# New durations and delays in the planner that orders an attention and mixer kernel

## The chip, the cores and the metric

The kernel runs on one core of a Trainium2 chip. The core has five engines with an instruction list each: TensorE (PE, matrix products, with its weight loads shown as PEld), VectorE (DVE), ScalarE (ACT), GpSimd (POOL) and SyncE (SP, which issues all transfers between memory and the core). An engine works through its list in order; a semaphore holds an instruction back until what it needs is there. The metric is the device time of one execution in microseconds (us). The kernel before took 1168.48 us, the median of three runs (1167.81 to 1168.57).

## The reference

Eight batches, eight heads, 576 positions, head size 64. The attention is block-causal: a query sees the keys of its own block of 64 and of the blocks before it.

```python
scores = (1/8) * q @ k^T, masked by blocks of 64      # per batch and head, 576 x 576
attn   = softmax(scores)
x      = attn @ v, heads side by side                 # 8 x 576 x 512
u      = x + (x^T @ U @ V)^T                          # U: 576 x 32, V: 32 x 576, over the positions
out    = u + relu(u @ w_ch1) @ w_ch2                  # w_ch1: 512 x 2048, w_ch2: 2048 x 512
```

U, V, w_ch1 and w_ch2 come as 64-bit floats (f64), q, k and v as 32-bit ones.

## The kernel before

**Stages.** A loop over the 64 heads writes the attention. A head is five tiles of up to 128 queries: products of queries and keys on PE (L1185 as full 32-bit products for heads 0 to 11, L1189 and L1190 as rounded products of two parts for the others), the row maximum on DVE (L1203), the exponential with its row sum on ACT (L1214), sum and reciprocal on DVE (L1230, L1231), the scaling on POOL (L1240), transposes on PE (L1273), a high part on ACT (L1250) and the rest on DVE (L1292, and L1299 which moves 64 partitions to the other 64), and the product with v on PE (L1316 for heads 0 to 9, L1332 later). The two halves of that product are added through a copy across partitions on ACT (L1338) and a sum on DVE (L1340). After every second head `mix` applies U and V (L1358 to L1408): transposes, splits (L1361, L1363), the product with U (L1372), a short chain over 32 partitions (L1375 to L1379), the product with V (L1387) and the sum u (L1392), which goes to memory.

Beside the heads run the conversion of the f64 weights and the feed-forward products. `split64` turns a block of 512 columns into 32-bit floats: a fetch, a magnitude on ACT (L359), a clamp on POOL (L362), then a shift (L338) and two joins of bits (L343, L351) on DVE. `weights_of` finds a common power of two by a short chain (`power`, L397 to L423) and writes high and low 16-bit halves (ACT L455, DVE L459). When the second half of w_ch2 is there, `agree` reconciles the scales (L482 to L488) and `level` rescales the first half (L499). `ffn_chunk` (288 tokens each) splits u (L596, L600, or L609, L614, L615), multiplies by the first half of the 2048 hidden columns (L631), applies the relu (L636, L639), multiplies by w_ch2 (L656) and adds (L668). These products are PE's stock of spare work: their priority number is over a million, the heads' at most 64 thousand, so PE takes them when no step of a head is ready.

The other 1024 hidden columns come last, in `block_products` (products L873), as two by two blocks with seven products in place of eight; their weights are made by L732, L737, L738 and L741, and the sums around the products are on DVE (L802, L810, L820, L827) and ACT (L801, L805, L834, L940).

**What sets the order.** Nothing is issued by hand. Each step is a task with an engine, an expected duration in ns, a priority, what it reads and what it writes. `Plan.issue` simulates the five engines with these numbers and writes each engine's list in the order of that simulation: a free engine takes, among the tasks whose inputs it believes ready, the one with the lowest priority number. The chip then follows the list, whatever the true times. A result of engine e reaches a task on another engine x after the duration, plus `TAIL[e]`, plus `INTO[x]`; on the same engine after 130 ns (for PE at once). DVE tasks marked `port` and all POOL tasks are never simulated at the same time. `_act`, `_dve` and `_pe` give a duration from the number of columns:

```python
TAIL = {"PE": 165, "DVE": 78, "ACT": 105, "POOL": 20, "SP": 0}
INTO = {"PE": 355, "DVE": 35, "ACT": 35, "POOL": 310, "SP": 60}
def _act(n, sbuf=False): return (93 if sbuf else 52) + 0.833 * n
def _dve(n): return 69 + 1.042 * n
```

In the trace a duration on DVE, ACT or POOL also holds the drain of the engine, which the planner counts as `TAIL`; an engine's next instruction can start during the drain of the last.

Of the kernel before, what the change touches and what calls it, by code (L numbers as in the profile page):

```python
# [53 lines left out]
INTO = {"PE": 355, "DVE": 35, "ACT": 35, "POOL": 310, "SP": 60}  # L54
# [192 lines left out]
def _dve(n):  # L247
    return 69 + 1.042 * n
# [13 lines left out]
def attention_then_mixer(  # L262
# [60 lines left out]
    def split64(fetches, shape, hi, lo, dst, prio, gate=(), part=slice(None), whole=None):  # L323
# [32 lines left out]
        if len(shape) > 2:  # L356
# [4 lines left out]
            "POOL", 250 + 0.85 * n, prio,  # L361
# [3 lines left out]
        add("DVE", 130 + 0.55 * n, prio, shift, [st, zt], [zt], port=True)  # L365
        add("DVE", 100 + 1.15 * n, prio, put_upper, [st, zt], [zt], port=True)
# [69 lines left out]
    def weights_of(half_bufs, hi, lo, blocks, scale, prio, limit=None):  # L436
# [15 lines left out]
        for n, b in enumerate(half_bufs["out"]):  # L452
# [5 lines left out]
                "DVE", 150 + 1.3 * CW, last,  # L458
# [15 lines left out]
    def agree(prio):  # L474
# [103 lines left out]
    def ffn_chunk(c, w, wb, fr=range(FC), turn=0):  # L578
# [12 lines left out]
        for k in range(KC):  # L591
            uh, ul = uh_r[k], ul_r[k]
            if not b:
                add(
                    "ACT", _act(T, True), E,
# [3 lines left out]
                    "DVE", _dve(T), E,  # L599
# [5 lines left out]
            else:  # L605
                us = take(us_r, "us")
                add(
                    "POOL", 250 + 0.85 * T, E,
# [6 lines left out]
                add("POOL", 780, E, lambda us=us, h=uh, l=ul: nc.gpsimd.tensor_sub(l.ap, us.ap, h.ap), [us, uh], [ul])  # L615
# [64 lines left out]
    def block_products():  # L680
# [38 lines left out]
        def weights(slots, by, sc):  # L719
# [15 lines left out]
            def halves(x, b):  # L735
                hi, lo, h, l = slots[x]
                add("ACT", _act(1024, True), L, lambda: nc.scalar.copy(hi(), w(b)), [b], [h])  # L737
                add("POOL", 60 + 2.3 * 1024, L, lambda: nc.gpsimd.tensor_sub(lo(), w(b), hi()), [b, h], [l])  # L738

            def total(out, x, y, op):  # L740
                add("POOL", 60 + 2.3 * 1024, L, lambda: getattr(nc.gpsimd, op)(w(out), w(x), w(y)), [x, y], [out])  # L741
# [54 lines left out]
        def piece(x, sc):  # L796
# [3 lines left out]
            if sc is None:  # L800
# [4 lines left out]
                "ACT", _act(2 * T, True), E, lambda: nc.scalar.activation(h.ap, x[0](), AF.Copy, scale=sc[:, 0:1]), [x[1], sc],  # L805
# [23 lines left out]
        def copied(out, x, iv=None):  # L829
            if iv is None:  # L830
# [3 lines left out]
                "ACT", _act(2 * T), E, lambda: nc.scalar.activation(out[0](), x[0](), AF.Copy, scale=iv.ap), [x[1], iv], [out[1]]  # L834
# [325 lines left out]
    def softmax(h, tiles, pr):  # L1160
# [37 lines left out]
        else:  # L1198
            add("PE", _pe(*ns, m=ms) + 40, pr, products, [q1, k1, q2, k2], [bank])
# [24 lines left out]
    def normalise(h, tiles, pr):  # L1224
# [9 lines left out]
        for i in tiles:  # L1234
# [4 lines left out]
                "POOL", 250 + 0.85 * w, pr,  # L1239
# [12 lines left out]
    def transpose(h, g, part, pr):  # L1252
# [41 lines left out]
        if m < n:  # L1294
# [3 lines left out]
                "DVE", _dve(64), pr,  # L1298
# [3 lines left out]
    def apply_v(h, g, pr):  # L1302
# [6 lines left out]
        if h < FP:  # L1309
# [11 lines left out]
            add("PE", cost + 15, pr, whole_products, [vr, *pt.parts], [bank], hold=[xb])  # L1321
# [15 lines left out]
        add("PE", cost + 80, pr, products, [vs, *ph.parts, *pl.parts], [bank], hold=[xb, tmp])  # L1337
        add("ACT", _act(n), pr, lambda: nc.scalar.copy(tmp[0:64, :n], bank[64:P, :n]), [bank], [tmp])  # L1338
# [5 lines left out]
    def mix(p, pr):  # L1344
# [3 lines left out]
        for rows, js in ((P, range(4)), (64, range(4, 5))):  # L1348
# [6 lines left out]
            def products(view=view, js=js, rows=rows):  # L1355
# [7 lines left out]
                "DVE", _dve(n * P), pr, lambda hi=hi, lo=lo, view=view: nc.vector.tensor_sub(lo, view(), f32(hi)),  # L1363
# [11 lines left out]
        add("ACT", _act(P), pr, lambda: nc.scalar.copy(tb.ap, low[R : 2 * R, 0:P]), [bank], [tb])  # L1375
        add("DVE", _dve(P), pr, lambda: nc.vector.tensor_add(tz.ap, low[0:R, 0:P], tb.ap), [bank, tb], [tz])
        add("ACT", _act(P, True), pr, lambda: nc.scalar.copy(t3[0:R, :], tz.ap), [tz], [t3])
        add("POOL", 360, pr, lambda: nc.gpsimd.tensor_sub(t3[R : 2 * R, :], tz.ap, f32(t3[0:R, :])), [tz, t3], [t3])
        add("ACT", _act(P, True), pr, lambda: nc.scalar.copy(t3[2 * R :, :], tz.ap), [tz], [t3])  # L1379
# [123 lines left out]
```

## Time and profile before

| | before |
|---|---|
| profiled execution, its own time | 1168.67 us |
| span of its trace | 1166.9 us |
| PE busy | 1135.2 us (97%) |
| DVE busy | 958.3 us (82%) |
| ACT busy | 794.0 us (68%) |
| POOL busy | 524.2 us (45%) |
| mean granted PE clock | 0.993 |

The span runs from the first to the last instruction; the execution's own time holds 1.8 us more around it. Busy times are unions of the recorded instructions. A PE that is busy in nearly all of the span can be shortened by filling its idle time alone, as long as its work stays the same. In the page, "out<-in" names the written and the read tiles without buffer numbers, "x" a count; in a row of the timeline the bracket gives the engine's idle time before the instruction and what ended it.

### The profile page before, as it was taken

The page shows a single profiled execution, that of the slowest core. Times are in us where ns is not written, and L with a number is a line of the kernel's source. Part 1 is how long each engine was busy: PE and PEld are TensorE (multiplying, and loading weights), DVE is VectorE, ACT ScalarE, POOL GpSimd, SP SyncE. Part 2 cuts the span into 40 slices and gives each one's busy share as a digit, 9 for nine tenths or more (in the row PEclk, how much of TensorE's full clock was granted, in tenths as well). Part 3 has the DMA queues.
Part 4 walks back from the last instruction along what each step waited for, and adds up shares of the span by engine and source line. Part 5 has one row for each costly group of instructions (what it writes and reads, how often), then busy time and mean ns, then how long its engine had stood idle before and what let it go on. Part 6 is the DMA issues. An engine that isn't in the chain of part 4 may idle for free.

```text
span 1166.9 us, 25406 instructions
## 1 busy us (share of the span) xinstructions
PE 1135.2 (97%) x9044; PEld 934.4 (80%) x9044; DVE 958.3 (82%) x2129; ACT 794.0 (68%) x1936; POOL 524.2 (45%) x696
## 2 busy tenths in 40 slices
PE   9999997999999999999999999999999999999998
PEld 7777776877888888888888887777777777777777
DVE  6899998889887878787878773372599999999998
ACT  7878887887898888888788954325345455554543
POOL 5445554876767685858576736737200000000000
PEclk9999997999999999999999999999999999999999
DMA  5454552735443434434433312241303422331321
GB/s 142 135 146 128 152 165 83 210 114 145 119 125 103 116 105 118 110 105 114 115 101 102 94 47 72 88 134 51 102 32 92 122 62 62 122 112 34 101 82 41
DMA packets 75885, 122.70 MB, mean 105 GB/s; under 512 B 8944, under 2 KB 52976, under 8 KB 75760
## 3 DMA queue, kind: packets, MB, share of 16 engines
q1 hardware_dynamic: 75760, 121.09, 36.4%
q8 instruction: 71, 1.16, 0.4%
q14 instruction: 54, 0.44, 0.1%
HBM read 76.23 MB, written 29.49 MB: 91 GB/s over the span
## 4 chain that ended last, share of the span: by engine, by line
PE 70%; DVE 13%; ACT 12%; issue 3%; POOL 1%; DMA 0%; SPq 0%; ACTq 0%; DVEq 0%; POOLq 0%
PE bb L873 28%; PE bf L656 9%; PE bf L631 8%; PE ba L1273 5%; ACT p L1214 5%; PE ba L1332 4%; PE bg L656 3%; PE bg L631 3%; DVE mx L1203 3%; DVE pl L1292 2%; PE ba L1316 2%; PE ba L1189 1%; ACT ph L1250 1%; PE ba L1190 1%; DVE xt L1340 1%
## 5 line engine op out<-in xcount | busy, mean ns | idle before, releaser
L1240 POOL TENSOR_SCALAR p<-p,rv 128x576 f32<-128x576 f32 (+4 forms) x320 | 170.6, 548 | 125.9 <-DVE rv L1231 91.6
L1273 PE MATMUL ba<-ident,p 128*128 128x128 f32 x768 | 123.1, 276 | 7.0 <-ACT p L1214 2.2
L1214 ACT ACTIVATE p<-ba,mx 128x448 f32<-128x448 f32 (+3 forms) x248 | 114.5, 465 | 22.3 <-DVE mx L1203 17.7
L1292 DVE TENSOR_TENSOR pl<-ba,ph 128x512 fp32r<-128x512 f32 x216 | 113.7, 550 | 14.8 <-ACT ph L1250 12.6
L656 PEld LDWEIGHTS <-w2h 128*128 128x128 f16 x1024 | 100.5, 98 | 29.7 <-issue 3.7
L873 PE MATMUL bb<-hh,w1l 128*128 128x288 f16 x448 | 118.9, 286 | 0.0
L873 PE MATMUL bb<-hh,w2h 128*128 128x288 f16 x448 | 118.9, 286 | 0.0
L873 PE MATMUL bb<-hh,w2l 128*128 128x288 f16 x448 | 118.9, 286 | 0.0
L873 PE MATMUL bb<-hh,w1h 128*128 128x288 f16 x448 | 118.9, 286 | 0.0
L656 PE MATMUL bf<-hh,w2h 128*128 128x288 f16 x408 | 118.2, 290 | 0.4 <-DVE ot L668 0.4
L631 PEld LDWEIGHTS <-w1h 128*128 128x128 f16 x1024 | 97.6, 98 | 25.5 <-issue 1.7
L656 PE MATMUL bf<-hl,w2h 128*128 128x288 f16 x408 | 117.3, 288 | 0.0
L656 PE MATMUL bf<-hh,w2l 128*128 128x288 f16 x408 | 117.3, 288 | 0.0
L801 ACT CAST hh<-hb 128x576 f16<-128x576 f32 x96 | 63.6, 666 | 66.8 <-DVE hb L827 43.0
L873 PEld LDWEIGHTS <-w1h 128*128 128x128 f16 x896 | 87.7, 98 | 22.0
L873 PEld LDWEIGHTS <-w2h 128*128 128x128 f16 x896 | 87.7, 98 | 22.0
L1250 ACT CAST ph<-ba 128x512 fp32r<-128x512 f32 x216 | 98.6, 493 | 9.6 <-PE ba L1273 8.1
L1273 PEld LDWEIGHTS ba<-ident,p 128*128 128x128 f32 x768 | 90.1, 142 | 13.7 <-issue 7.8
L1203 DVE TENSOR_REDUCE mx<-ba 128x1 f32<-128x448 f32 (+3 forms) x248 | 94.1, 405 | 4.7 <-PE ba L1190 3.2
L1332 PE MATMUL ba<-ph,vs 128*128 128x256 f32 (+3 forms) x432 | 93.2, 272 | 1.8 <-DVE pl L1292 1.5
L873 PE MATMUL bb<-hl,w2h 128*128 128x288 f16 x448 | 91.6, 286 | 0.0
L873 PE MATMUL bb<-hl,w1h 128*128 128x288 f16 x448 | 91.6, 286 | 0.0
(193 smaller groups left out, 3197.0 us busy)
## 6 DMA issues: line engine op xcount, KB each, us to landing
raw<-in_qk_dram SPq DMA_DIRECT2D x63, 288.0 KB, 3.9
st<-in_w_dram SPq DMA_DIRECT2D x32, 512.0 KB, 3.8
o_d<-ot SPq DMA_DIRECT2D x72, 144.0 KB, 1.8
vr<-in_v_dram SPq DMA_DIRECT2D x32, 320.0 KB, 3.8
ur<-u_d SPq DMA_DIRECT2D x64, 144.0 KB, 2.5
wr<-o_d SPq DMA_DIRECT2D x32, 288.0 KB, 3.1
out_dram<-wr SPq DMA_DIRECT2D x31, 288.0 KB, 2.3
ur<-u_d SPq DMA_DIRECT2D x30, 288.0 KB, 3.2
```

Source lines behind the costliest of these rows:

```text
L631: nc.tensor.matmul(ps[:, :T], w()[wn][:, k, fs], m[k].ap, start=(i == 0), stop=(i == len(ops) - 1))
L656: nc.tensor.matmul(ps[:, :T], w()[wn][:, f, ms], hs[f][x].ap, start=(i == 0), stop=(i == len(ops) - 1))
L801: add("ACT", _act(2 * T, True), E, lambda: nc.scalar.copy(h.ap, x[0]()), [x[1]], [h])
L873: nc.tensor.matmul(bank[:, i, :T], x()[:, w(k)], p.ap[:, k, :], start=first and n == 0, stop=last and n == len(ops) - 1)
L1203: lambda i=i, at=at: nc.vector.tensor_reduce(out=mx[: P if i else 64, i : i + 1], in_=view(i, at), op=ALU.max, axis=AX.XY if wide else AX. ...
L1214: nc.scalar.activation(out.rearrange("p (j k) -> p j k", j=2) if wide else out, view(i, at), AF.Exp, bias=mx[:rows, i : i + 1], accum_out= ...
L1240: lambda x=x, rows=rows, i=i: nc.gpsimd.tensor_scalar(out=x, in0=x, scalar1=rv[:rows, i : i + 1], scalar2=1.0, op0=ALU.mult, op1=ALU.mult),
L1250: add("ACT", _act(n), pr, lambda: nc.scalar.copy(out(), inp()), reads, writes)
L1273: nc.tensor.transpose(out=bank[:, a : a + P], in_=pt_r[i][h % PB[i]][:, j * P : (j + 1) * P], identity=perm.ap)
L1292: "DVE", _dve(m), pr, lambda: nc.vector.tensor_sub(pl[:, low], bank[:, :m], f32(ph[:, low])), [bank, bh], [bl]
L1316: nc.tensor.matmul(bank[:, a:n], vr[:, x : x + 2, :], pt[:, _at(g, j)], start=(j == 0), stop=(j == NK[g] - 1))
L1332: nc.tensor.matmul(bank[0 : c.stop, a:n], vs[:, j, c], x[:, _at(g, j)], start=(i == 0), stop=(i == len(ops) - 1))
```

## The change

Only numbers that the planner reads are changed: two delays and the expected durations of some thirty kinds of tasks. What the instructions compute, their number, the buffers and the priorities stay.

```diff
-INTO = {"PE": 355, "DVE": 35, "ACT": 35, "POOL": 310, "SP": 60}
+INTO = {"PE": 355, "DVE": 60, "ACT": 60, "POOL": 200, "SP": 60}
...
-            "POOL", 250 + 0.85 * n, prio,                              # clamp, L362
+            "POOL", 145 + 0.85 * n, prio,
-        add("DVE", 130 + 0.55 * n, prio, shift, ...)                   # L338
-        add("DVE", 100 + 1.15 * n, prio, put_upper, ...)               # L343
+        add("DVE", 50 + 0.55 * n, prio, shift, ...)
+        add("DVE", 13 + 1.15 * n, prio, put_upper, ...)
-            "DVE", 150, prio,                                          # reduction in power, L397
+            "DVE", 65, prio,
-            "DVE", 150, prio,                                          # multiply, L428
+            "DVE", 70, prio,
-                "DVE", 150 + 1.3 * CW, last,                           # low half, L459
+                "DVE", 1.3 * CW, last,
-        add("DVE", 500, prio, limits, [a, b, c], [d, joint])           # L482 to L484
+        add("DVE", 1700, prio, limits, [a, b, c], [d, joint])
-                    "ACT", _act(2 * CW, True), -1.0,                   # level, L499
+                    "ACT", _act(2 * CW, True) + 100, -1.0,
-                    "ACT", _act(T, True), E,                           # L596
+                    "ACT", _act(T, True) + 94, E,
-                    "DVE", _dve(T), E,                                 # L600
+                    "DVE", _dve(T) + 60, E,
-                    "POOL", 250 + 0.85 * T, E,                         # L609; likewise the scaling, L1240
+                    "POOL", 235 + 0.85 * T, E,
-                add("POOL", 780, E, ...)                               # L615
+                add("POOL", 692, E, ...)
-                    "ACT", _act(1024, True), L,                        # L732
+                    "ACT", _act(1024, True) + 105, L,
-                add("POOL", 60 + 2.3 * 1024, L, ...)                   # L738 and L741
+                add("POOL", 60 + 1.98 * 1024, L, ...)
-                "ACT", _act(2 * T, True), E, ...                       # L805; L834 likewise
+                "ACT", _act(2 * T, True) + 105, E, ...
-            add("PE", _pe(*ns, m=ms) + 40, pr, products, ...)          # L1189, L1190
+            add("PE", _pe(*ns, m=ms) + (90 if wide else 50), pr, products, ...)
-                "DVE", _dve(64), pr,                                   # across partitions, L1299
+                "DVE", _dve(64) + 112, pr,
-            add("PE", cost + 15, pr, whole_products, ...)              # L1316
+            add("PE", cost + 115, pr, whole_products, ...)
-        add("PE", cost + 80, pr, products, ...)                        # L1332
-        add("ACT", _act(n), pr, ...)                                   # across partitions, L1338
+        add("PE", cost + 110, pr, products, ...)
+        add("ACT", _act(n) + 125, pr, ...)
-                "DVE", _dve(n * P), pr, ...                            # L1363
+                "DVE", _dve(n * P) + (112 if rows == 64 else 0), pr, ...
-        add("ACT", _act(P), pr, ...)                                   # L1375
+        add("ACT", _act(P) + 120, pr, ...)
-        add("POOL", 360, pr, ...)                                      # L1378
-        add("ACT", _act(P, True), pr, ...)                             # L1379
+        add("POOL", 545, pr, ...)
+        add("ACT", _act(P, True) + 120, pr, ...)
```

More of the change, by code (lines that the diff above doesn't have):

```diff
@@ L364, in split64 @@
         )
-        add("DVE", 130 + 0.55 * n, prio, shift, [st, zt], [zt], port=True)
-        add("DVE", 100 + 1.15 * n, prio, put_upper, [st, zt], [zt], port=True)
+        add("DVE", 50 + 0.55 * n, prio, shift, [st, zt], [zt], port=True)
+        add("DVE", 13 + 1.15 * n, prio, put_upper, [st, zt], [zt], port=True)
         if whole:
@@ L804, in piece @@
             add(
-                "ACT", _act(2 * T, True), E, lambda: nc.scalar.activation(h.ap, x[0](), AF.Copy, scale=sc[:, 0:1]), [x[1], sc],
+                "ACT", _act(2 * T, True) + 105, E, lambda: nc.scalar.activation(h.ap, x[0](), AF.Copy, scale=sc[:, 0:1]), [x[1], sc],
                 [h],
@@ L833, in copied @@
             add(
-                "ACT", _act(2 * T), E, lambda: nc.scalar.activation(out[0](), x[0](), AF.Copy, scale=iv.ap), [x[1], iv], [out[1]]
+                "ACT", _act(2 * T) + 105, E, lambda: nc.scalar.activation(out[0](), x[0](), AF.Copy, scale=iv.ap), [x[1], iv], [out[1]]
             )
@@ L1320, in apply_v @@
             cost = sum(5 + 1.667 * (n - max(P * j - q0, 0)) for j in range(NK[g]))
-            add("PE", cost + 15, pr, whole_products, [vr, *pt.parts], [bank], hold=[xb])
+            add("PE", cost + 115, pr, whole_products, [vr, *pt.parts], [bank], hold=[xb])
             copy(False, n, pr, lambda: xt[me, q0:q1], lambda: bank[0:64, :n], [bank], [xb])
@@ L1336, in apply_v @@
         cost = _pe(*(n - max(P * j - q0, 0) for *_, j in ops), m=[c.stop for _, c, _ in ops])
-        add("PE", cost + 80, pr, products, [vs, *ph.parts, *pl.parts], [bank], hold=[xb, tmp])
-        add("ACT", _act(n), pr, lambda: nc.scalar.copy(tmp[0:64, :n], bank[64:P, :n]), [bank], [tmp])
+        add("PE", cost + 110, pr, products, [vs, *ph.parts, *pl.parts], [bank], hold=[xb, tmp])
+        add("ACT", _act(n) + 125, pr, lambda: nc.scalar.copy(tmp[0:64, :n], bank[64:P, :n]), [bank], [tmp])
         add(
@@ L1362, in mix @@
             add(
-                "DVE", _dve(n * P), pr, lambda hi=hi, lo=lo, view=view: nc.vector.tensor_sub(lo, view(), f32(hi)),
+                "DVE", _dve(n * P) + (112 if rows == 64 else 0), pr,
+                lambda hi=hi, lo=lo, view=view: nc.vector.tensor_sub(lo, view(), f32(hi)),
                 [bank, xh], [xl, xh] if rows == 64 else [xl],
```

16 lines of the change are left out of this document (8 added, 8 removed).

## The prediction

> **What bounds the kernel now.** I read the page first, then busy times by stage, then the stage in which TensorE (PE) stops, engine by engine in order of time. The page:
>
> ```profile
> span 1166.9 us, 25406 instructions
> ...
> PE 1135.2 (97%) x9044; PEld 934.4 (80%) x9044; DVE 958.3 (82%) x2129; ACT 794.0 (68%) x1936; POOL 524.2 (45%) x696
> ...
> PEclk9999997999999999999999999999999999999999
> ...
> PE 70%; DVE 13%; ACT 12%; issue 3%; POOL 1%; DMA 0%; SPq 0%; ACTq 0%; DVEq 0%; POOLq 0%
> ```
>
> PE is busy for 1135.2 of 1166.9 us, so 31.7 us of idle time are all that a better order could fill, apart from stretches at a lower clock. The chain that ended last is PE for 70% and VectorE (DVE) for 13%. The clock row shows one bad slice, the seventh (175 to 204 us).
>
> The next view gives each stage its busy time: start and end, length, then PE, PEld, DVE, ACT and POOL, and at the end the granted clock, DMA share and GB/s.
>
> ```profile
> 0.00:60.00 60.00, 57.32 (x318) 46.65 (x319) 45.49 (x142) 46.18 (x129) 29.28 (x58) 1.00 0.48 135
> 60.00:180.00 120.00, 111.75 (x810) 90.90 (x809) 114.09 (x285) 98.10 (x266) 62.09 (x87) 0.99 0.53 152
> 180.00:300.00 120.00, 109.72 (x863) 91.55 (x863) 106.19 (x263) 98.92 (x261) 80.72 (x107) 0.94 0.46 131
> 300.00:720.00 420.00, 412.75 (x3442) 351.64 (x3440) 324.68 (x880) 342.82 (x952) 285.22 (x391) 1.00 0.38 106
> 720.00:834.00 114.00, 114.00 (x930) 90.61 (x929) 47.48 (x98) 41.25 (x77) 66.94 (x56) 1.00 0.29 87
> 834.00:1164.00 330.00, 329.63 (x2691) 263.06 (x2689) 320.17 (x465) 166.73 (x254) 0.00 (x0) 1.00 0.26 78
> ```
>
> The reader should see four stages. Up to 60 us PE idles 2.7 us. From 60 to 300 us it idles 8.25 + 10.28 = 18.5 us, while DVE is busy for 114.09 and 106.19 of each 120: here the weights are converted beside the attention heads, and DVE is the bound. From 300 to 720 us PE idles 7.25 us. From 720 us on it is idle for 0.4 us until its last product, so no order of instructions can shorten that part; it can only lengthen it. I therefore work out what the change does to the 28.4 us up to 720 us.
>
> The largest holes of PE, with what ended them in brackets:
>
> ```profile
> 89.33 3.51 PE L1316 MATMUL ba<-pw,vr 128*128 128x256 f32 x10 [2.53 <-ACT pw L1250]
> ...
> 184.87 0.47 PE L1273 MATMUL ba<-swap,p 128*128 128x128 f32 x1 [2.02 <-DVE xt L1340]
> ...
> 191.75 0.74 PE L1332 MATMUL ba<-ph,vs 128*128 128x256 f32 x2 [1.48 <-DVE pl L1292]
> ...
> 197.74 0.73 PE L1273 MATMUL ba<-ident,p 128*128 128x128 f32 x4 [1.73 <-DVE tz L1376]
> ```
>
> They are 2.53 + 2.02 + 1.48 + 1.73 = 7.8 us, three of them behind DVE and one behind ScalarE (ACT). Around the same places the clock is halved:
>
> ```profile
> 88.90:92.30 3.40, 2.97 (x7) 2.43 (x8) 3.37 (x6) 2.60 (x7) 1.49 (x3) 0.50 0.00 0
> 184.50:194.70 10.20, 8.17 (x39) 6.34 (x40) 8.96 (x32) 7.41 (x14) 4.04 (x5) 0.50 0.47 130
> 198.20:201.50 3.30, 3.30 (x16) 2.25 (x14) 2.80 (x6) 3.20 (x9) 2.21 (x2) 0.50 0.00 0
> ```
>
> Read the second and the clock column: in 198.2 to 201.5 PE is busy for all of 3.30 us at 0.50, so it did 1.65 us' work in 3.30. A half-clock stretch of about 3.4 us thus costs 1.65 us where PE is busy throughout; the long one costs at most half its 8.17 busy us, 4.1.
>
> The Trainium skill, "TensorE: Matmul & The Clock Gate" (Part 1: The HAM clock gate), says that the clock is halved after an idle window of about 3.4 us. The longest hole above is 2.53 us and the clock fell all the same, so I go by the trace: short holes close together suffice. By the rule no hole here would ever cost clock, term (c) below would be 0, and the sum 1165.5.
>
> **The change part by part.** No instruction, buffer, transfer, priority or semaphore rule is added or removed. The only thing that changes is a table of expected durations and delays, by which the planner simulates the engines and writes each engine's list. What can move is the order in those lists, and which free buffer each step gets. So every instruction keeps its own cost: PE's work is the same, and each term is a difference in waiting.
>
> The transfers that SyncE (SP) issues are ordered by the same simulation and may be issued a little earlier or later; among PE's waits one alone is put down to a transfer:
>
> ```profile
> PE bw L1189 <- DMA k<-k: 1.3, 1, 1.3
> ```
>
> So I cost that queue at nothing, up to this 1.3 us either way.
>
> Are the new numbers nearer to the trace? Three checks. First the shift of 64 partitions:
>
> ```profile
> 322.16 0.22 DVE L1299 TENSOR_TENSOR ph<-ba,ph 64x64 fp32r<-64x64 f32 x1
> 322.41 0.49 DVE L1292 TENSOR_TENSOR pl<-ba,ph 128x320 fp32r<-128x320 f32 x1
> ```
>
> Start to start it takes 0.25 us; the planner had 69 + 1.042 x 64 = 136 ns and gets 248. Then the release of GpSimd (POOL) by DVE:
>
> ```profile
> 182.88 0.18 DVE L1231 RECIPROCAL rv<-rv 128x3 f32<-128x3 f32 x1
> ...
> 183.16 1.22 POOL L1240 TENSOR_SCALAR p<-p,rv 128x320 f32<-128x320 f32 x3 [0.93 <-DVE rv L1231]
> ```
>
> DVE ends at 183.06, POOL starts at 183.16, 0.10 us after the recorded end. The planner adds 78 ns of tail (which the recorded duration already holds) and 310, now 200: still later than the row, but nearer. And two groups of the late stage:
>
> ```profile
> L741 POOL TENSOR_TENSOR wr<-wr 128x1024 f32<-128x1024 f32 x8 | 18.8, 2354 | 0.2
> L732 ACT ACTIVATE wr<-wr,sc 128x1024 f32<-128x1024 f32 x8 | 9.1, 1147 | 0.1
> ```
>
> The ACT step with a scale per partition takes 1147 ns where the plan had 946 and gets 1051; a recorded duration contains the drain that the plan adds apart (105 for ACT), so the new figure fits. The POOL sums take 2354 where the plan had 2415 and gets 60 + 1.98 x 1024 = 2088: this one gets worse. It lies between 720 and 834 us, where PE never waits, and I cost it at nothing; the cover is the feed-forward products of other tokens, and without it eight sums at 0.27 us would be 2.1 us.
>
> *(a) The f64 steps on DVE.* The rows below are of 0 to 300 us, the second number after the bar being the mean ns of one:
>
> ```profile
> L351 DVE SCALAR_TENSOR_TENSOR wr<-st,z 128x512 int32<-128x512 int32 x22 | 19.6, 890 | 0.1
> L343 DVE SCALAR_TENSOR_TENSOR z<-st,z 128x512 int32<-128x512 int32 x22 | 18.8, 856 | 0.2
> L338 DVE TENSOR_SCALAR z<-z 128x512 int32<-128x512 int32 x23 | 11.2, 492 | 0.2
> L459 DVE SCALAR_TENSOR_TENSOR w2l<-wr,sc,w2h 128x512 f16<-128x512 f32 x8 | 7.1, 921 | 0.1
> L459 DVE SCALAR_TENSOR_TENSOR w1l<-wr,sc,w1h 128x512 f16<-128x512 f32 x8 | 6.5, 857 | 0.0
> ```
>
> The same steps when nothing disturbs them (start, duration):
>
> ```profile
> 79.64 0.68 DVE L351 SCALAR_TENSOR_TENSOR wr<-st,z 128x512 int32<-128x512 int32 x1
> 85.48 0.41 DVE L338 TENSOR_SCALAR z<-z 128x512 int32<-128x512 int32 x1
> 86.12 0.67 DVE L343 SCALAR_TENSOR_TENSOR z<-st,z 128x512 int32<-128x512 int32 x1
> ...
> 192.84 0.74 DVE L459 SCALAR_TENSOR_TENSOR w2l<-wr,sc,w2h 128x512 f16<-128x512 f32 x1
> ```
>
> The excess over these is 22 x (890 - 680) + 22 x (856 - 670) + 23 x (492 - 410) + 8 x (921 - 740) + 8 x (857 - 740) ns = 4.6 + 4.1 + 1.9 + 2.4 = 13.0 us of DVE time. What makes it is seen here, one DVE step and what POOL did meanwhile:
>
> ```profile
> 280.21 3.09 DVE L343 SCALAR_TENSOR_TENSOR z<-st,z 128x512 int32<-128x512 int32 x1
> ...
> 279.99 1.40 POOL L1135 TENSOR_TENSOR q<-raw,q 64x576 fp32r<-64x576 f32 x1
> 281.35 1.39 POOL L1136 TENSOR_TENSOR k<-raw,k 64x576 fp32r<-64x576 f32 x1
> ```
>
> The step begins beside one POOL operation and gets through only after the next one too, 3.09 us for 0.67. The planner never lets these two run together, but nothing enforces that on the chip; overlap comes when its clock and the chip's drift apart. With true durations there should be less drift. I take a third of 13.0, 4.3 us of DVE time. How much reaches PE? DVE's 13% of the chain are 152 us of its 45.49 + 114.09 + 106.19 + 324.68 + 47.48 = 638 busy us before 834, so 0.24 on average; since PE's idle share is 18.5/240 in this stage against 7.25/420 in the next, I take 0.4. Term: -1.7 us. Bounds: -5.2 (all of 13.0 at 0.4), and above nothing, the second rival.
>
> The Trainium skill, "SBUF — State Buffer" (SBUF: two separate sides), says that a DVE operation with two SBUF inputs and a POOL one that reads SBUF exclude each other, whoever starts first holding the port for its whole instruction. By that the step would wait for the first POOL operation alone (until 281.39) and take 1.85 us. It took 3.09: DVE lost to the second as well. By the rule a third of the 1.24 us between, at 0.4, falls out of the term: 1164.9.
>
> *(b) The six-instruction limit step,* 500 ns in the plan and now 1700. It starts at 189.43 and the next DVE work at 191.22:
>
> ```profile
> 189.43 0.34 DVE L482 SCALAR_TENSOR_TENSOR joint<-sc 128x1 f32<-128x1 f32 x1
> 189.81 0.67 DVE L483 SCALAR_TENSOR_TENSOR joint<-joint,sc 128x1 f32<-128x1 f32 x1
> ...
> 191.15 0.15 DVE L484 COPY sc<-joint 128x1 f32<-128x1 f32 x1
> 191.22 0.48 DVE L1292 TENSOR_TENSOR pl<-ba,ph 128x320 fp32r<-128x320 f32 x1
> ```
>
> So 1700 is right. But it cannot be broken up, and what waits behind it (the split L1292, on which PE's 1.48 us hole hangs) waits still. Gain at most that hole, loss at most the 1.2 us by which other work is now put off; I take -0.3.
>
> *(c) The clock.* The three stretches are some five periods of 3.4 us. If holes of 60 to 300 us get shorter, one falls out in about half the cases: -0.8 of 1.65. Bounds -6 (all: 1.5 + 4.1 + 1.65 is 7.2, less overlap with waits) and +1.65 for a new one.
>
> *(d) 300 to 720 us.* The shifts (L1299, L1338, L1363, L1375, L1379), PE costs 10 to 100 ns longer, and the 25 ns longer release of DVE and ACT all make the plan later, towards the trace. PE, which takes its list in order, is then less often given a step whose input is late while feed-forward products could run. Of 7.25 us I take a sixth, -1.2; bounds -7.25 and, if the new order is merely another one, as much again upward, nearer to the small end since PE has spare products here.
>
> Sum: -1.7 - 0.3 - 0.8 - 1.2 = -4.0. The profiled execution took 1168.67 us (its span and 1.8 around it); that gives **1164.7**. The median of the runs is 1168.48, 0.2 lower, so against it this is -3.8 us or 0.32%. About 0.2% (2.3 us) is what a measurement of this kernel can tell from nothing.
>
> **The rivals.** *Nothing measurable.* The list is a priority list; most steps keep their place, and a few swaps gain here and lose there. For it: from 300 us on PE is 98% busy. Against it: 18.5 us idle in a stage whose costs change most. 1168.5, chance 0.20.
>
> *Slower: the plan becomes too hopeful about DVE.* In 0 to 300 us it books 22 x (80 + 87) + 16 x 150 ns = 6.1 us less for the f64 steps, 1.2 more for the limits: 4.9 us less, while the means above are 13.0 over the undisturbed ones. If POOL keeps disturbing them as often, the old padded figures were nearer to the mean, and PE will be handed transposes and products whose DVE half is not done, in front of fillers that could run. Price: 4.9 at 0.4 is 2.0, and a new half-clock period, 1.65: 1172.3. It decides if L343 still averages above 0.80 us. For it: a third gain in overlap is only hoped for. Chance 0.32.
>
> *Much faster: the holes at 87 and 183 to 198 us close.* These 7.8 us and the long half-clock stretch (4.1) are 11.9; three quarters give 1159.7. It needs conversions spread so that spare products are left when w2's second half is converted; nothing in the table aims at it. Chance 0.10.
>
> **How the numbers follow.** The forecast itself (1161.5 to 1167.5) has 0.38, of which I count 0.02 as too small to measure. Faster: 0.36 + 0.10 = 0.46; same 0.22; slower 0.32. Cases of both signs hold much of the chance, so the range runs from below the much faster case, 1158, to above the slower one, 1174, for (c) and (d) have open upper ends.
>
> **What would show it.** (a) the means of L343 and L351 in 0 to 300 us fall below 0.80; still above 0.85 says the second rival. (c) PEclk in 60 to 300 us: a fourth stretch, or one fewer. (d) PE's idle time in 300 to 720 us, 7.25 now, nearer to 6. From 720 to 1164 PE must stay at full; idle time there would make everything above wrong, since DVE is busy for 320 of 330 us in the last stage and an order that delays its sums has little slack.

## The result and the profile after

The kernel with the new table takes 1148.71 us (median of four runs, 1148.11 to 1150.22), beside 1168.53 for the kernel before in four: 19.8 us less, ratio 0.9829, 95% interval 0.9812 to 0.9846. I had forecast 1164.7 with a range from 1158 to 1174. The sign was that of the forecast; the size was five times as large and lies outside the range. The profiled execution took 1148.11 us. Its page, in the lines that answer to those shown of before:

```profile
span 1146.3 us, 25411 instructions
...
PE 1120.8 (98%) x9044; PEld 929.5 (81%) x9044; DVE 954.7 (83%) x2129; ACT 791.7 (69%) x1936; POOL 525.7 (46%) x696
...
PEclk9999999999999999999999999999999999999999
...
PE 74%; DVE 14%; ACT 6%; issue 2%; POOL 2%; DMA 1%; SPq 0%; ACTq 0%; DVEq 0%; POOLq 0%
```

PE's idle time went from 31.7 to 1146.3 - 1120.8 = 25.5 us. That is 6.2 us of the 20.6 by which the span fell. The other 14.4 us came out of PE's *busy* time, 1135.2 before and 1120.8 now, with the same 9044 products. Part of it is the clock. One half-clock stretch is left in place of three:

```profile
191.90:195.30 3.40, 3.19 (x13) 2.04 (x14) 3.21 (x10) 3.33 (x11) 0.90 (x2) 0.50 0.02 5
```

Before, PE was busy for 2.97 + 8.17 + 3.30 = 14.4 us at 0.50, now for 3.19; half of the difference, 5.6 us, is what the clock gave at most. So at least 8.8 us remain in which PE was recorded as busy and did no work. Where, is told by the counts of products in the busy-time view. First before, then after, 60 to 300 and 300 to 660 us (the number after PE's busy time is the count):

```profile
60.00:300.00 240.00, 221.47 (x1671) 182.46 (x1670) 220.28 (x547) 197.03 (x526) 142.81 (x193) 0.96 0.50 141
300.00:660.00 360.00, 353.41 (x2942) 302.00 (x2940) 287.61 (x784) 307.72 (x861) 254.83 (x349) 1.00 0.41 111
```

```profile
60.00:300.00 240.00, 224.79 (x1739) 185.99 (x1738) 226.13 (x582) 203.96 (x541) 153.96 (x205) 0.99 0.52 151
300.00:660.00 360.00, 357.83 (x3044) 311.79 (x3042) 288.15 (x781) 310.34 (x875) 258.38 (x356) 1.00 0.40 111
```

From 300 to 660 us PE is 98.2% busy before and 99.4% after, a difference of 4.4 us. Yet it got through 3044 products in place of 2942. At 360 us / 2942 = 0.12 us each the 102 products are 12 us; 74 of them are the spare products L656 (589 before, 663 after). From 60 to 300 us it is 68 products more, 9.8 us at 240 / 1671. Together these rough figures are about the whole gain; from 660 us on both kernels only finish what is left of the same work.

That the hidden part is waiting, and not slower products, follows from the start times in the traces. As an estimate, take for each pair of kinds of product that follow each other the lower quartile of the time from start to start (over before, after and the runs reflected and padded below) as undisturbed. Then the products of 300 to 660 us are 325.1 us of work before and 337.2 after, and the time beyond that falls from 35.0 to 22.9 us: idle time from 6.6 to 2.2, time hidden in records from 28.4 to 20.7. Of the hidden part, 12.3 us stands before products that wait for no semaphore, in both kernels; before products that do wait it falls from 16.1 to 8.4.

What hides in the busy time is seen in the kernel before around 444.7 us, PE first, then ACT:

```profile
444.59 0.29 PE L656 MATMUL bf<-hh,w2l 128*128 128x288 f16 x1
444.72 0.29 PE L656 MATMUL bf<-hl,w2h 128*128 128x288 f16 x1
445.00 0.50 PE L1387 MATMUL ba<-v,t 96*128 96x288 f32 x2
```

```profile
444.56 0.29 ACT L1379 CAST t<-tz 32x128 fp32r<-32x128 f32 x1
444.88 0.68 ACT L1132 ACTIVATE raw<-raw 64x576 f32<-64x576 f32 x1
```

A product is recorded for 0.29 us, but the next one starts 0.12 later (444.59, 444.72). After the second row PE starts again at 445.00: 0.28 us later, of which 0.16 are waiting, and no bracket shows idle time because the record of the last product reaches to 445.01. What PE waits for is L1379 of ACT, whose record ends at 444.85. That is one of the steps across partitions whose start-to-start time, 0.32 us here, the old table had 120 ns too short. This error alone did not make the hole, though: by the old table PE gets the result 200 + 105 + 355 = 660 ns after the start of L1379, on the chip it had it after 0.44 us. PE was free 0.28 us after that start (444.84), so against the plan the chain lagged some 0.4 us behind PE's list; which earlier steps added up to this was not followed. A hole of up to 0.17 us is invisible as idle time.

The idle time that the profile does show in this stage, by what ended it (us, times, longest), before and after:

```profile
PE ba L1273 <- ACT p L1214: 1.7, 5, 0.4
PE ba L1387 <- ACT p L1214: 0.9, 2, 0.7
PE ba L1387 <- DVE xt L1340: 0.5, 1, 0.5
PE ba L1387 <- ACT t L1379: 0.4, 1, 0.4
```

```profile
PE ba L1273 <- ACT p L1214: 0.6, 2, 0.4
PE ba L1189 <- ACT p L1214: 0.3, 1, 0.3
PE ba L1388 <- ACT p L1214: 0.2, 1, 0.2
```

The product with V (L1387, L1388 after the change, since the new file has one line more above it) no longer shows a wait for L1379 or L1340.

### The profile page after: what moved, and what is told of

The parts are those of the page before. It is cut to its first block, busy times and chain, and to the rows that moved or that the text cites. A ratio compares the mean times of both kernels' runs of the same rounds, so it can differ in the third digit from the quotient of the medians.

```text
span 1146.3 us, 25411 instructions
## 1 busy us (share of the span) xinstructions
PE 1120.8 (98%) x9044; PEld 929.5 (81%) x9044; DVE 954.7 (83%) x2129; ACT 791.7 (69%) x1936; POOL 525.7 (46%) x696
## 4 chain that ended last, share of the span: by engine, by line
PE 74%; DVE 14%; ACT 6%; issue 2%; POOL 2%; DMA 1%; SPq 0%; ACTq 0%; DVEq 0%; POOLq 0%
PE bb L873 29%; PE bf L656 11%; PE bf L631 9%; PE ba L1273 7%; PE ba L1332 5%; PE bg L631 3%; ACT p L1214 3%; DVE mx L1203 3%; PE bg L656 2%; DVE pl L1292 2%; PE ba L1190 2%; PE ba L1189 2%; PE ba L1316 1%; PE ba L1358 1%; DVE wr L351 1%
## 5 line engine op out<-in xcount | busy, mean ns | idle before, releaser
L1214 ACT ACTIVATE p<-ba,mx 128x448 f32<-128x448 f32 (+3 forms) x248 | 114.5, 466 | 21.3 <-DVE mx L1203 19.1
L656 PEld LDWEIGHTS <-w2h 128*128 128x128 f16 x1024 | 100.5, 98 | 31.0 <-issue 3.5
L656 PE MATMUL bf<-hh,w2h 128*128 128x288 f16 x416 | 120.1, 289 | 2.5 <-ACT w2h L455 2.2
L1292 DVE TENSOR_TENSOR pl<-ba,ph 128x512 fp32r<-128x512 f32 x216 | 113.6, 549 | 10.4 <-ACT ph L1250 8.4
L656 PE MATMUL bf<-hh,w2l 128*128 128x288 f16 x416 | 119.6, 287 | 0.5 <-DVE w2l L459 0.5
L656 PE MATMUL bf<-hl,w2h 128*128 128x288 f16 x416 | 119.5, 287 | 0.0
L1250 ACT CAST ph<-ba 128x512 fp32r<-128x512 f32 x216 | 99.8, 492 | 9.3 <-PE ba L1273 7.6
```

The lines of the kernel that those rows point to most:

```text
L656: nc.tensor.matmul(ps[:, :T], w()[wn][:, f, ms], hs[f][x].ap, start=(i == 0), stop=(i == len(ops) - 1))
L1214: nc.scalar.activation(out.rearrange("p (j k) -> p j k", j=2) if wide else out, view(i, at), AF.Exp, bias=mx[:rows, i : i + 1], accum_out= ...
L1250: add("ACT", _act(n), pr, lambda: nc.scalar.copy(out(), inp()), reads, writes)
L1292: "DVE", _dve(m), pr, lambda: nc.vector.tensor_sub(pl[:, low], bank[:, :m], f32(ph[:, low])), [bank, bh], [bl]
```

## The experiments

Only numbers in the planner's table differ between the kernels. Each time is a median, and each ratio goes against runs of before on the same chip in the same hour (1167.0 to 1167.6 us).

**Is it luck?** A list scheduler can turn a tiny change of a number into another order throughout. Nudges of both tables:

```diff
-"DVE": 35, "ACT": 35     # before
+"DVE": 36, "ACT": 36     # before_1ns
+"DVE": 37, "ACT": 37     # before_37
-"DVE": 60, "ACT": 60     # after
+"DVE": 61, "ACT": 61     # after_1ns
+"DVE": 62, "ACT": 62     # after_62
```

> The table of before with one meaningless nudge: delay into DVE and ACT 36 in place of 35 ns. Luck theory (any nudge reshuffles the lists, and the new kernel is a lucky draw): the time leaves 1168.5 by 5 us or more, either way. Fit theory (the gain comes from numbers nearer to the truth): within 3 us of 1168.5.

> The table of after with the same nudge: 61 in place of 60 ns. Luck theory: the gain of 19.8 us is mostly lost, 1156 or more. Fit theory: within 3 us of 1148.7.

> Before with 37 in place of 35 ns into DVE and ACT, which moves the order of all engines from the start (the nudge to 36 moved the later part only). Lucky draw alone: somewhere in 1148 to 1168, with no tie to 1168. Fit alone: within 3 us of 1168. Both (a spread of about ten us between equally good tables, and a better mean for the new one): 1160 to 1172.

> After with 62 in place of 60 ns into DVE and ACT. Lucky draw alone: as for the nudged before. Fit alone: within 3 us of 1148.7. Both: 1148 to 1160, nearer to 1157.4, where the nudge to 61 came out, than to 1148.7.

Measured: 1167.23 us (ratio 0.9997, 0.9984 to 1.0009) and 1167.61 (0.9997, 0.9987 to 1.0006) for the tables of before; 1157.37 (0.9906, 0.9891 to 0.9922) and 1148.01 (0.9836, 0.9821 to 0.9851) for those of after. So neither theory alone holds. One nudge in two costs after 8.7 us; the better table still has the better mean: 1151.4 over its three orders against 1167.8 over the three of before, 16 us. Inside a kernel the scatter is larger than the times show. The order with 37 ns is as fast as before, but by another way:

```profile
60.00:300.00 240.00, 227.36 (x1731) 189.31 (x1730) 220.45 (x576) 203.46 (x546) 153.54 (x205) 0.97 0.50 148
300.00:660.00 360.00, 348.93 (x2881) 297.53 (x2879) 286.47 (x776) 308.70 (x861) 251.87 (x345) 1.00 0.39 109
```

From 60 to 300 us it has 60 products more than before, from 300 to 660 us 61 fewer.

Part of what the nudge to 61 ns cost is clock. The kernel with 61 has four half-clock stretches, three of them at places where after has none:

```profile
84.80:88.20 3.40, 3.40 (x13) 2.61 (x13) 3.11 (x11) 2.96 (x9) 0.65 (x2) 0.50 0.00 1
187.20:190.60 3.40, 3.40 (x17) 2.68 (x15) 3.33 (x9) 3.02 (x10) 0.43 (x1) 0.50 0.00 0
217.90:221.30 3.40, 3.40 (x22) 2.93 (x22) 3.06 (x8) 3.33 (x11) 2.32 (x6) 0.51 0.19 65
542.20:545.60 3.40, 3.40 (x16) 2.37 (x17) 1.73 (x5) 2.97 (x10) 0.14 (x1) 0.50 0.10 31
```

They hold 13.6 busy us against 3.19 in after; half of the difference, 5.2 of the 8.7 us, is what the clock took at most.

**Which numbers?** Delays, shifts and weight steps alone on before, and all but one group:

```diff
 # delays_alone: before with
+INTO = {"PE": 355, "DVE": 60, "ACT": 60, "POOL": 200, "SP": 60}
 # without_delays: after with
+INTO = {"PE": 355, "DVE": 35, "ACT": 35, "POOL": 310, "SP": 60}
 # shifts_alone: before with
+_dve(64) + 112            # L1299
+_act(n) + 125             # L1338
+_dve(n * P) + (112 if rows == 64 else 0)   # L1363
+_act(P) + 120, 545, _act(P, True) + 120    # L1375, L1378, L1379
 # weights_alone: before with the new numbers of L362, L338, L343, L397, L428, L459, limits, L499, L596, L600
 # without_weights: after with the old numbers of these
```

> Before with the new delays alone (into DVE and ACT 60, into POOL 200). If the delays carry the gain, since they enter every step of every head: 1155 or less. If the durations carry it: 1163 or more.

> After with the old delays (35, 35, 310), all new durations kept. If the delays carry the gain: 1163 or more. If the durations carry it: 1155 or less. If both parts add up, this and the run with the delays alone lose and gain together 19.8 us.

> Before with the new costs of steps across partitions and of the short chain on 32 partitions alone (L1299, L1338, L1363, L1375, L1378, L1379). If these carry the durations' part, since each lies in every head or pair of heads: about 1157. If the weight steps carry it: 1165 to 1169.

> Before with the new costs of the f64 and weight steps alone (L362, L338, L343, L397, L428, L459, the limits, L499, L596, L600). My forecast put most of the gain here, in 0 to 300 us: then about 1160. By the second rival (plan too hopeful about DVE) 1170 or more. If the other groups carry the gain: 1165 to 1169.

> After with the old costs of the f64 and weight steps. If the loss of 2.6 us that they gave alone on before adds up, this is faster than after: about 1146. If the groups only work together: slower than 1152.

Measured: delays alone 1160.48 us (0.9934, 0.9920 to 0.9949); all but the delays 1157.02 (0.9903, 0.9885 to 0.9920); shifts alone 1154.56 (0.9893, 0.9878 to 0.9907); weight steps alone 1170.79 (1.0024, 1.0009 to 1.0040); all but the weight steps 1155.49 (0.9893, 0.9870 to 0.9915). The weight steps, on which my forecast put most, gain nothing by themselves. The shifts, to which I gave a part of 1.2 us, give 12.9 of 1167.5. That the weight steps help within the whole (1155.49 without, 1148.71 with) is less than the 8.7 us that a nudge of 1 ns moved after, and is not settled. The new PE costs and the POOL and ACT numbers of the late stage were not tried alone.

Then the shifts one by one:

```diff
 # act_copy_alone: before with
+_act(n) + 125             # L1338
 # dve_shift_alone: before with
+_dve(64) + 112            # L1299
 # mix_chain_alone: before with
+_dve(n * P) + (112 if rows == 64 else 0)   # L1363
+_act(P) + 120, 545, _act(P, True) + 120    # L1375, L1378, L1379
```

> Before with the ACT copy across partitions (L1338, 108 times) 125 ns longer in the plan, and nothing else. The shifts together gave 12.9 us. If what counts is how much hidden time of one engine the plan regains (108 x 125 = 13.5 us of ACT, against 6.0 of DVE for L1299 and some 0.5 us per pair of heads in the chain), this one carries most: 1160 or less. If what counts is a step with PE directly behind it: 1165 or more here, since after L1338 a DVE sum comes first.

> Before with L1299 (54 times) 112 ns longer in the plan, and nothing else. Engine-time theory: about 1163. Step-before-PE theory: 1160 or less, since PE's product L1332 needs it at once.

> Before with the chain of the mixing step alone (L1363 +112, L1375 +120, L1378 360 to 545, L1379 +120). Engine-time theory: 1164 or more, for it runs only 32 times. Step-before-PE theory: 1162 or less, since two products L1387 wait for its end and the plan had it too short by 0.4 us.

Measured: 1161.83 us (0.9956, 0.9941 to 0.9971), 1174.61 (1.0071, 1.0053 to 1.0090) and 1162.85 (0.9958, 0.9941 to 0.9975). Against 1166.98 this is -5.2, +7.6 and -4.1, together -1.7, where the three at once gave -12.9. The parts do not add up, so neither of the two theories (engine time, step before PE) can be read from them: a single entry moves less than the scatter between orders.

**Does the direction count?** For this the whole table was moved along one line, the change being one unit of it, and one was made later only:

```diff
 # reflected: each number = before - (after - before), e.g.
+INTO = {"PE": 355, "DVE": 10, "ACT": 10, "POOL": 420, "SP": 60}
+_act(n) + -125            # L1338
 # halfway: each number = before + 0.5 * (after - before), e.g.
+INTO = {"PE": 355, "DVE": 47.5, "ACT": 47.5, "POOL": 255, "SP": 60}
 # twice: each number = before + 2 * (after - before), e.g.
+INTO = {"PE": 355, "DVE": 85, "ACT": 85, "POOL": 90, "SP": 60}
 # padded: before with
+INTO = {"PE": 355, "DVE": 135, "ACT": 135, "POOL": 310, "SP": 60}
```

> Every number of before moved by the same amount the other way (into DVE and ACT 10, into POOL 420, L1338 125 ns shorter, and so on): twice as far from the truth. Theory that nearness to the truth counts: 1175 or more. Theory that any table is one draw among equals and before was a bad draw: 1150 to 1165. Theory that only later (padded) tables help: 1175 or more as well.

> Every number half way between before and after. Nearness to the truth: 1155 to 1162. One draw among equals: anywhere from 1148 to 1175.

> Every number moved twice as far: past the truth by as much as before fell short of it. Nearness to the truth: about as slow as before, 1160 to 1172. Theory that later costs for shifts, PE and delays help by padding, whatever the truth: 1145 or less.

> Before with 100 ns more into DVE and ACT (135 in place of 35) and nothing else; the trace has some 25 more. Padding theory: 1155 or less, as PE would be given spare products first. Nearness to the truth: no better than the 1160.5 of the new delays, 1160 to 1172.

Measured: reflected 1189.75 us (1.0191, 1.0176 to 1.0206), halfway 1152.67 (0.9871, 0.9855 to 0.9888), twice 1153.41 (0.9879, 0.9864 to 0.9893), padded 1156.99 (0.9907, 0.9893 to 0.9922). The reflected table loses 22 us, more than twice the 8.7 us of the nudges. That speaks against luck among equals, though it is one order, not nudged, and no pure mirror: the limits step gets 500 - 1200 = -700 ns, a duration that nothing can have. Its stages and those of the padded table:

```profile
60.00:300.00 240.00, 210.77 (x1547) 171.58 (x1547) 209.56 (x517) 185.73 (x489) 138.20 (x180) 0.94 0.46 135
300.00:660.00 360.00, 348.77 (x2896) 298.50 (x2895) 284.62 (x775) 305.02 (x846) 253.38 (x344) 1.00 0.39 111
```

```profile
60.00:300.00 240.00, 218.26 (x1657) 179.60 (x1656) 220.77 (x554) 195.88 (x515) 142.47 (x191) 0.97 0.49 143
300.00:660.00 360.00, 356.67 (x3017) 309.29 (x3015) 286.87 (x780) 311.42 (x871) 258.39 (x356) 1.00 0.40 112
```

The padded table is further from the trace in its delays than before, and still wins 10.5 us. By the counts nearly all of it comes after 300 us: 3017 products for 2942 there, 1657 for 1671 from 60 to 300 us. So lateness can help in that stage without being true; this too is one order, not nudged.

How true the later numbers of after are, the trace of before can tell, and "some 25 more" is not what it shows. Where DVE or ACT, idle for over 0.15 us, was released by another engine within 0.4 us (562 starts), it began 36 ns after that engine's recorded end in the median and 50 in the mean. The old 35 was the usual case, and the new 60 is in good part padding. The same holds for the shifts. The copy L1338 with 256 columns:

```profile
L1338 ACT COPY tmp<-ba 64x256 f32<-64x256 f32 x54 | 20.0, 370 | 11.8 <-PE ba L1332 10.5
```

The old table had 265 ns and a tail of 105: together the recorded 370, so the result was already expected at the right time, and is now expected 125 ns too late. What the old table had too short is the time until ACT's next step. Where that follows within 60 ns, it starts on average 346 ns after the copy for 256 columns (42 cases) and 372 for 320 (52 cases); the plan had 265 and 319 and gets 390 and 444, nearer for the first and farther for the second. So truth and lateness are mixed in the change, and no run here separates them.

**Nearer still, and later still.** The last two start from after:

```diff
 # refined: after with
-add("DVE", 100 + 1.15 * n, prio, put_lower      # L351
+add("DVE", 13 + 1.15 * n, prio, put_lower
-60 + 1.98 * 1024                                # L741
+60 + 2.2 * 1024
-add("POOL", 820, pr, lambda: nc.gpsimd.tensor_sub(lo, mine   # L1158
+add("POOL", 850, pr, lambda: nc.gpsimd.tensor_sub(lo, mine
-add("DVE", 150, prio, lambda: nc.vector.tensor_copy(sc.ap    # L423
+add("DVE", 70, prio, lambda: nc.vector.tensor_copy(sc.ap
 # after_padded: after with
+INTO = {"PE": 355, "DVE": 135, "ACT": 135, "POOL": 200, "SP": 60}
```

> After with four more numbers brought to the trace: L351 from 689 to 602 ns for 512 columns, the POOL sums L741 from 2088 to 2313, L1158 from 820 to 850, the copy of the scale L423 from 150 to 70. Nearness to the truth: 1140 to 1148, the gain before 300 us, where these steps lie, and PE's count in 60 to 300 us at 1750 or more. Scatter between equal tables: 1148 to 1158.

> After with 135 in place of 60 ns into DVE and ACT. Two-stage theory (later is better from 300 us on, where spare products are, and truth is better before, where DVE is the bound): PE's count in 300 to 660 us 3040 to 3060 against 3044, in 60 to 300 us at most 1742, and the time 1148 to 1156. If padding helped everywhere: 1145 or less.

Measured: refined 1153.05 us (0.9877, 0.9860 to 0.9894), after_padded 1146.24 (0.9822, 0.9799 to 0.9845). Four more numbers moved towards the trace gained nothing beyond the scatter. The padded one is the fastest median here, but its interval overlaps that of after (0.9812 to 0.9846), so it is not shown to beat it. Its stages:

```profile
60.00:300.00 240.00, 222.69 (x1738) 184.95 (x1737) 223.82 (x578) 202.99 (x546) 153.80 (x206) 0.99 0.50 149
300.00:660.00 360.00, 359.02 (x3069) 314.36 (x3068) 286.56 (x779) 307.73 (x867) 254.17 (x348) 1.00 0.39 110
```

All runs in one table, with the counts of PE's products from the same view as above:

| kernel | median us | 60 to 300 us | 300 to 660 us |
|---|---|---|---|
| reflected | 1189.75 | 1547 | 2896 |
| dve_shift_alone | 1174.61 | 1648 | 2918 |
| weights_alone | 1170.79 | 1637 | 2953 |
| before | 1168.53 | 1671 | 2942 |
| before_37 | 1167.61 | 1731 | 2881 |
| before_1ns | 1167.23 | 1675 | 2953 |
| mix_chain_alone | 1162.85 | 1692 | 2949 |
| act_copy_alone | 1161.83 | 1706 | 2949 |
| delays_alone | 1160.48 | 1711 | 2974 |
| after_1ns | 1157.37 | 1697 | 2987 |
| without_delays | 1157.02 | 1697 | 3002 |
| padded | 1156.99 | 1657 | 3017 |
| without_weights | 1155.49 | 1739 | 3015 |
| shifts_alone | 1154.56 | 1678 | 3036 |
| twice | 1153.41 | 1686 | 3051 |
| refined | 1153.05 | 1725 | 3016 |
| halfway | 1152.67 | 1741 | 3001 |
| after | 1148.71 | 1739 | 3044 |
| after_62 | 1148.01 | 1738 | 3038 |
| after_padded | 1146.24 | 1738 | 3069 |

In 300 to 660 us the tables of before (2881 to 2953) and those of after (2987 to 3069 with the padded and the refined) do not overlap, and the count rises all along the line: 2896, about 2925 (mean of three), 3001, about 3023 (mean of three), 3051. From 60 to 300 us the families overlap (1671 to 1731 against 1697 to 1739); only the reflected table stands clearly apart. Work can move from one stage to the other, as with 37 ns, so one count alone is a weak witness; the larger the sum of the two, the shorter is the time, with few exceptions. That truth matters there, as DVE is the bound, was my theory for the last two runs; refined did not bear it out, and it stays open.

## Why the prediction was wrong

**What bounds the kernel.** The step that failed is the first one: "31.7 us of idle time are all that a better order could fill". PE's busy time is a union of records of 0.29 us that start 0.12 us apart, so it counts holes of up to 0.17 us as work. At least 8.8 us of the gain came from there, behind the visible 6.2 and at most 5.6 of clock. The same step made me read "from 300 us on PE is 98% busy" as a stage with 7.25 us to gain. Of the 16.0 us by which the forecast was off, some 10.8 lie in term (d), which rests on this, and up to 4.8 in term (c).

**The single numbers** (shift, release of POOL) stand as read: the new ones are nearer to the rows shown. But the shift row compares the time from start to start alone. L1299 is recorded for 0.22 us, and the old plan had 136 + 78 = 214 ns until its result: right before, 112 ns late now. And the "25 ns longer release of DVE and ACT" in term (d) leads mostly past the trace, not towards it. What I drew from the shift row was too small, too: 54 steps L1299 by 112 ns are 6.0 us of DVE, 108 copies L1338 by the 81 and 53 ns of the trace 7.2 us of ACT, and the 32 chains come on top. Together this is more than the 6.1 us that the f64 steps were changed by, and the forecast gave it a share of term (d).

**(a) f64 steps.** -1.7 us forecast, from a third less disturbance. The same rows after:

```profile
L343 DVE SCALAR_TENSOR_TENSOR z<-st,z 128x512 int32<-128x512 int32 x26 | 21.8, 842 | 0.2
L351 DVE SCALAR_TENSOR_TENSOR wr<-st,z 128x512 int32<-128x512 int32 x24 | 18.2, 760 | 0.1
L338 DVE TENSOR_SCALAR z<-z 128x512 int32<-128x512 int32 x26 | 12.5, 495 | 0.1
L459 DVE SCALAR_TENSOR_TENSOR w1l<-wr,sc,w1h 128x512 f16<-128x512 f32 x8 | 6.0, 779 | 0.0
L459 DVE SCALAR_TENSOR_TENSOR w2l<-wr,sc,w2h 128x512 f16<-128x512 f32 x8 | 5.7, 743 | 0.4 <-ACT w2h L455 0.3
```

The excess over the undisturbed rows is 26 x (842 - 670) + 24 x (760 - 680) + 26 x (495 - 410) + 8 x (779 - 740) + 8 x (743 - 740) ns = 4.5 + 1.9 + 2.2 + 0.3 + 0.0 = 8.9 us, 4.1 less than the 13.0 of before, as forecast (4.3). L351 fell below the 0.80 that the prediction had named, L343 with 0.84 stayed between its two marks, and the new numbers of these steps alone made the kernel 0.24% slower (1.0009 to 1.0040). So the disturbance fell with the order as a whole; that it pays 0.4 us per us was not shown. The second rival had the sign of this group right (it gave +3.6, measured about +3), and was wrong as a forecast for the whole; but 3 us is less than a nudge can move.

**(b) The limits.** Not tried alone. Of the four holes that I listed, none is there in its old place, but new ones of like size are. PE's longest waits in 60 to 300 us after (us, times, longest):

```profile
PE bf L656 <- ACT w2h L455: 2.2, 1, 2.2
PE ba L1273 <- ACT xt L1250: 2.0, 1, 2.0
PE bw L1185 <- ACT p L1214: 1.6, 1, 1.6
```

So the much faster rival had the size (1159.7) closer than the forecast, but not the way: the large holes moved, and did not close.

**(c) The clock.** -0.8 forecast for one period fewer; four fewer, up to 5.6 us. The way was right, the term mis-sized: I took one chance in two for one period. That shorter holes brought it about is not shown. After still has this hole, behind which the clock stayed full, while 1.73 us at 197.74 in before had half clock behind it:

```profile
103.62 0.52 PE L1273 MATMUL ba<-ident,p 128*128 128x128 f32 x3 [1.99 <-ACT xt L1250]
```

The number of stretches also changes with a nudge, from one to four between 60 and 61 ns, so part of this gain may be luck.

**(d) 300 to 720 us.** -1.2 forecast, about 12 measured up to 660 us by the count of products (4.4 of it visible as idle time). The reason given there, PE takes its list in order and is given fewer steps whose input is late, agrees with the waits: the hidden time before waiting products fell from 16.1 to 8.4 us, the idle time of 300 to 720 us from 7.25 to 2.2. The size failed because its base was the visible 7.25 us. The bound, too: I set -7.25 as the most that the stage could give.

**From 720 us on** I said PE must stay at full. It did not quite:

```profile
720.00:834.00 114.00, 113.07 (x921) 89.73 (x920) 63.62 (x116) 44.48 (x80) 49.27 (x42) 1.00 0.29 87
```

```profile
798.93 0.65 PE L631 MATMUL bf<-uh,w1h 128*128 128x288 f16 x4 [0.93 <-DVE hl L639]
```

One hole of 0.93 us at 798 us, nine products fewer than the 930 of before. It costs about a microsecond, and nothing like what I feared.

**Nothing measurable** was given 0.20 on the ground that swaps cancel. For the tables of before they do (three orders within 1.3 us); across the two families they don't.

## What to carry to other kernels

Before taking a busy share as a bound, divide: count the instructions in a stage and compare with the start-to-start time of undisturbed ones; where records overlap, short waits vanish from the idle time. In a planner for an engine that takes its list in order and has spare work, an input believed too early can cost a wait each time, while one believed too late leaves the engine its spare work: here the padded delays won 10.5 us. A rule for each single number it is not: 112 ns more on L1299 alone lost 7.6 us. Compare a number with both times that the planner draws from it, when the engine is free and when the result is there. And judge a table by several nudged orders, not by one: here a change of 1 ns moved a kernel by 8.7 us, more than any single entry did.

## What the runs showed of the hardware that was not expected

**A step across partitions starts on an empty engine, and can hold the next one.** The timeline of ACT in the kernel before; L1375 copies partitions 32 to 63 to 0 to 31, L1377 in the same chain stays where it is:

```profile
84.69 0.66 ACT L359 ACTIVATE z<-st 128x512 f32<-128x512 f32 x1
85.38 0.26 ACT L1375 COPY tb<-ba 32x128 f32<-32x128 f32 x1
85.66 0.42 ACT L1214 ACTIVATE p<-ba,mx 128x192 f32<-128x192 f32 x1
...
86.07 0.71 ACT L455 ACTIVATE w2h<-wr,sc 128x512 f16<-128x512 f32 x1
86.69 0.28 ACT L1377 CAST t<-tz 32x128 fp32r<-32x128 f32 x1
86.87 1.94 ACT L455 ACTIVATE w2h<-wr,sc 128x512 f16<-128x512 f32 x3
```

L1377 starts 0.09 us before the record of its predecessor ends (86.78), and its successor 0.10 before its own ends (86.97). L1375 starts 0.03 after its predecessor's end (85.35), and its successor 0.02 after its own (85.64). So the overlap of about 0.1 us is lost at both ends here. Over the whole trace, where the predecessor ended no more than 60 ns earlier, L1375 (25 times) and L1379 (32) start 24 ns behind its end in the median, L1377 (22) 101 ns before it. The far end depends on what comes next. Behind the copy L1338, which reads PSUM from partition 64 on, the 42 steps that read PSUM from partition 0 on (L1214, L1250, L1361) and two that are shifted themselves (L1375, L1379) start after its end. The 39 that read SBUF, without a shift, and the 11 that are again L1338 start before it.

DVE does the same with L1299, beside the two rows in the prediction:

```profile
321.18 0.95 DVE L1292 TENSOR_TENSOR pl<-ba,ph 128x448 fp32r<-128x448 f32 x2
...
322.82 0.75 DVE L1203 TENSOR_REDUCE mx<-bw 128x1 f32<-128x576 f32 x1
```

L1299 starts at 322.16, behind the end at 322.13, and L1292 follows at 322.41, behind 322.38; the reduction after that starts 0.08 before L1292 ends (322.90). In the median it is 31 ns on either side of L1299 (54 and 51 times). The Trainium skill, "VectorE: DVE Perf Modes" (Two Vector instructions with no wait between them), gives as a model that an instruction whose output starts in another group of 32 partitions than the last output into the same memory starts only when every earlier one has finished. The DVE rows agree, and by it the step behind the shift must wait too, as it does. For ACT these rows and counts alone speak.

**Half clock after a hole of 2.2 us.** PE in the kernel after, ahead of the stretch from 191.90 to 195.30:

```profile
188.84 0.29 PE L656 MATMUL bf<-hl,w2h 128*128 128x288 f16 x1
191.33 0.30 PE L656 MATMUL bf<-hh,w2h 128*128 128x288 f16 x1 [2.21 <-ACT w2h L455]
192.11 0.42 PE L656 MATMUL bf<-hh,w2l 128*128 128x288 f16 x1 [0.49 <-DVE w2l L459]
192.33 0.45 PE L656 MATMUL bf<-hl,w2h 128*128 128x288 f16 x1
```

The record of the same product grows from 0.29 to 0.45 us behind it. The Trainium skill, "TensorE: Matmul & The Clock Gate" (Part 1: The HAM clock gate), has the clock halved after an idle window of about 3.4 us; as with the stretches of before, a shorter hole was enough here. Its length alone does not decide: the hole of 1.99 us at 103.62 left the clock full. What else decides was not tried.
